# Reciprocal denominators expanded on TensorE instead of through DRAM, and transposes placed inside the key products

## The chip, the cores and the metric

The kernel runs on one core of a Trainium2 chip. The metric is the device time of one execution in microseconds; the number given for a kernel is the median of its runs. The engines are TensorE (PE in the profile; its weight loads are PEld), VectorE (DVE), ScalarE (ACT), GpSimd (POOL) and SyncE (SP), which here only issues DMAs.

## What is computed

x has 2048 rows (tokens) of 640 features. It is normalised over the features, and two branches read the result xn. Branch A is a linear attention with 32 heads of 20 features; branch B is a two-layer network with 1728 hidden units. The output is x + A * silu(B). The reference, cut to what matters:

```python
def A(xn, wqkv, wo):                       # S = 2048, D = 640, H = 32, Dh = 20
    q, k, v = split(xn @ wqkv)             # heads
    phi = lambda t: where(t > 0, t + 1, exp(t)) + 1e-6
    pq, pk = phi(q), phi(k)
    kv  = einsum("bhsd,bhse->bhde", pk, v)
    z   = einsum("bhsd->bhd", pk)
    num = einsum("bhqd,bhde->bhqe", pq, kv)
    den = einsum("bhqd,bhd->bhq", pq, z)[..., None] + 1e-6
    return merge_heads(num / den) @ wo
def B(xn, w1, w2):
    return maximum(xn @ w1, 0) @ w2
xn = layernorm(x)
out = x + A(xn, wqkv, wo) * silu(B(xn, w1, w2))
```

## The kernel before

Every operation is recorded by a small scheduler, `Sched`, in the order in which the Python code issues it. Each engine runs its own instructions strictly in that order. A wait is put in front of an operation where it reads what another engine or a DMA wrote, or overwrites what another still reads. There is no planner: where a call stands in the code is where its instructions stand on each engine. All DMAs go through SP's queue, in order too.

The work goes in these stages.

Start. Token tiles (128 rows, `t`) are loaded, `LN_stats` and `LN_norm` normalise them on VectorE into `xn`. Tiles 0 to 3 are transposed on TensorE against an identity (`transposes`, five products, line 413) and copied from PSUM by ScalarE (`xnT_copy`, line 418); tiles 4 to 15 are transposed by DMA. `K_mm(t, b)` (line 430) makes the keys of a tile: two halves of 320 columns (`a`), five contraction steps (`k`), ten products into the PSUM banks b and b+1. With a list of steps `ks` it issues only those, both halves of a step next to each other. `K_exp`, `K_relu` (ScalarE) and `K_fin` (VectorE) turn the keys into `pk`. `warm(n)` issues n small products whose result nobody reads.

Main loop. For each of four chunks of 512 tokens (`j`), 5 query blocks (line 482, 5 products of 512 columns, evicted into `pqT`) and 13 hidden blocks (line 505, likewise, into `hT`), in a ring of six PSUM banks; among them the stats, norms and key products of the next chunk's tiles. The last 64 hidden units are made by `H_half` (line 518) into `hTl`: chunk 2jp lies on partitions 0 to 63, chunk 2jp+1 on 64 to 127. POOL sums `pk` into `zacc` (line 442). In chunk 3 follow `z_split`, `z_col` after block n = 7 and `den` after block n = 9: `den` makes all denominators in one bank, with 20 products of line 593 that each use 32 columns of the array, so head h of chunk i lies on partition 32 i + h. VectorE adds 1e-6 (line 597) and takes reciprocals (line 601) into `rden`.

Reciprocals. `den` then stores `rden` to a DRAM scratch `rxd`, every head's row 20 times (4 DMAs, line 605). After the weights of the second layer, five DMAs (line 666) load it back by feature into `rx`, which takes the room of `xnT`. `divide(m)` (line 678) multiplies one block of 128 features of `pqT` by it on VectorE, for all 2048 tokens at once.

Second part. `G_block(k)` makes xn.T @ pk (32 products of 320 columns each, line 685; five blocks, banks 0 to 3), copied by ScalarE into `GT`. `kv_block` (line 697) multiplies by the value weights and VectorE masks off what lies outside the heads, into `kvp`, which POOL clears before (line 812). `W_block(m)` (line 712) folds the output weights in, into `wf`; its left half is evicted by ScalarE (line 716), its right half by VectorE (line 718).

Then the second layer `U(p)` for eight pairs of token tiles (line 751, two halves `n` of 320 output columns, 26 products each) and `s_tile(t)` (line 779, 10 products), which makes branch A's result of one tile. The last 64 hidden units enter by products of 64 rows (line 729), in which the two tiles of a pair use the two row halves of the array. They are issued eight at a time: four that end pair p (even), four that begin pair p+1. So the odd pairs end in full products, and Silu (line 747) of their first half can go as soon as that half is done. Silu writes `g_sb`, which lies in `xnT`'s room, and so also waits for the `divide`s that read there (`divs`). `ubanks` gives even pairs banks 4 to 7 and odd ones 0 to 3. A `hook` between the halves of U issues other work: kv in pair 0, W in pair 1, from then on the `s_tile`s of the pair two before; pair 7's hook issues those of pairs 5 and 6. The last pair's two tiles come at the end. VectorE multiplies by `g_sb` (line 793) and adds x (line 796), and SP stores the tile (line 799). A tile is one piece of 640 columns, or two of 320 with `last=True`, as both last tiles are.

Of the kernel before, what the change touches and what calls it, by code (L numbers as in the profile page):

```python
# [211 lines left out]
def bass_recurrent_scan__linear_attn_block__dense_activation_relu__prompt_kernel(  # L212
# [74 lines left out]
    ek = nc.alloc_sbuf_tensor("ek", [P, NEK, 2, D], bf)  # L287
    er = nc.alloc_sbuf_tensor("er", [P, NER, 2, 512], bf)
    ident = nc.alloc_sbuf_tensor("ident", [P, P], bf)
    mh = nc.alloc_sbuf_tensor("mh", [P, C, H], f32)  # L290
    zmat = nc.alloc_sbuf_tensor("zmat", [P, C, H], bf)
    zacc = nc.alloc_sbuf_tensor("zacc", [P, D], f32)
# [12 lines left out]
    rx = xnT  # L305
    rxd = nc.dram_tensor("rden_by_feature", [D, S], bf).ap()

    psT = nc.alloc_psum_tensor("psT", [P, 8 * 512], f32)
    ps = [psT[:, 512 * i:512 * (i + 1)] for i in range(8)]
# [60 lines left out]
    warm(36)  # L370

    def build_consts():
        sc.op("POOL", lambda eng: eng.memset(mh[:, :, :], 1.0), W=[("mh",)])
# [52 lines left out]
    def K_mm(t, b, ks=None):  # L426
        fns = []
        for a, k in ([(a, k) for a in range(2) for k in range(C)] if ks is None else [(a, k) for k in ks for a in range(2)]):
            if True:
                fns.append(lambda eng, a=a, k=k: eng.matmul(  # L430
                    ps[b + a][:, 0:HN], lhsT=xnT[:, k, tok(t)], rhs=wqk[:, k, D + HN * a:D + HN * (a + 1)],
                    start=(k == 0), stop=(k == C - 1)))
        wks = [0, 1] if ks is None else [0 if ks[0] < KS else 1]
# [120 lines left out]
    K_relu(1, 2)  # L554
    LN_stats(4)
    K_fin(0)
    K_mm(2, 0)
    K_exp(2, 0)
    K_relu(2, 0)
    LN_stats(5)  # L560
# [27 lines left out]
    def den():  # L588
# [76 lines left out]
    for c in range(C):  # L665
        dma("SP", lambda eng, c=c: eng.dma_start(rx[:, c, :], rxd[P * c:P * (c + 1), :]),
            R=[("rxd", i) for i in range(J)], W=[("rx", c)], extra=[lastW1])


    pr = [0]  # L670
# [3 lines left out]
        pr[0] += 1  # L674
        return b

    def divide(m):
        return sc.op("DVE", lambda eng: eng.tensor_tensor(out=pqT[:, m, :], in0=pqT[:, m, :], in1=rx[:, m, :], op=ALU.mult),  # L678
                     R=[("rx", m)] + [("pqT", i, m) for i in range(J)], W=[("pqT", i, m) for i in range(J)])

    def G_block(k, b):
        fns = []
# [23 lines left out]
    def W_block(m):  # L706
        b = nextp()
        cs = cs_of_m(m)
        fns = []
        for a in range(2):  # L710
            for ci, c in enumerate(cs):
                fns.append(lambda eng, a=a, c=c, ci=ci: eng.matmul(  # L712
                    ps[b + a][:, 0:HN], lhsT=kvp[:, c, P * m:P * (m + 1)], rhs=wo_sb[:, c, HN * a:HN * (a + 1)],
                    start=(ci == 0), stop=(ci == len(cs) - 1)))
        sc.group("PE", fns, R=[("wo",), ("kvz",)] + [("kv", c) for c in cs], W=[("ps", b), ("ps", b + 1)])
        sc.op("ACT", lambda eng: eng.activation(out=wf[:, m, 0:HN], in_=ps[b][:, 0:HN], func=ACTF.Copy),
              R=[("ps", b)], W=[("wf", m, 0)])
        sc.op("DVE", lambda eng: eng.tensor_copy(wf[:, m, HN:D], ps[b + 1][:, 0:HN]),
              R=[("ps", b + 1)], W=[("wf", m, 1)])

    pairs = [(4 * jj + q, 4 * jj + q + 4) for jj in (0, 2) for q in range(4)]

    def ubanks(p):
        return [4, 6] if p % 2 == 0 else [0, 2]

    def U_half(p, start):
        bs = ubanks(p)
        jp, q = pairs[p][0] // 8, pairs[p][0] % 4
        return [(lambda eng, u=u, n=n: eng.matmul(  # L729
            ps[bs[n] + u][:, 0:HN], lhsT=hTl[64 * u:64 * (u + 1), jp, P * q:P * (q + 1)],  # L730
            rhs=w2l[64 * u:64 * (u + 1), HN * n:HN * (n + 1)], start=start, stop=not start))
            for n in range(2) for u in range(2)]

    def U(p, hook):
        t0, t1 = pairs[p]
        bs = ubanks(p)
        odd = p % 2 == 1
        jp = t0 // 8
        Rh = [("hT", t // 4, f) for t in (t0, t1) for f in range(NF)] + [("w2", 0), ("w2", 1)]
        Rl = [("hTl", 0), ("hTl", 1), ("w2l", 0), ("w2l", 1)]  # L740

        def bk(n):
            return [("ps", bs[n]), ("ps", bs[n] + 1)]

        def silu(n):
            go = g_sb[:, t0:t0 + 5:4, HN * n:HN * (n + 1)]
            sc.op("ACT", lambda eng: eng.activation(out=go, in_=ps2(bs[n], HN), func=ACTF.Silu),  # L747
                  R=bk(n), W=[("g", t0, n), ("g", t1, n)], extra=[divs[c] for c in sorted({v // S for t in (t0, t1) for v in (D * t, D * t + D - 1)})])

        for n in range(2):  # L750
            fns = [(lambda eng, u=u, t=t, f=f, n=n: eng.matmul(  # L751
                ps[bs[n] + u][:, 0:HN], lhsT=hT[:, f, tok(t)], rhs=w2_sb[:, f, HN * n:HN * (n + 1)],
                start=(f == 0 and not odd), stop=(f == NF - 1 and odd)))
                for u, t in enumerate((t0, t1)) for f in range(NF)]
            if n == 0 or odd:
                sc.group("PE", fns, R=Rh, W=bk(n))
                sc.allow_unread.update(bk(n))
                if odd:
                    silu(n)
            else:  # L760
                sc.group("PE", fns + U_half(p, False), R=Rh + Rl, W=bk(0) + bk(1))
                b2 = ubanks(p + 1)
                W2 = [("ps", b2[i] + u) for i in range(2) for u in range(2)]
                sc.group("PE", U_half(p + 1, True), R=Rl, W=W2)
                sc.allow_unread.update(W2)
                silu(0)
                silu(1)
            if n == 0:
                hook()

    so = [0]

    def s_tile(t, last=False):
# [4 lines left out]
        for a in range(2):  # L778
            sc.group("PE", [(lambda eng, c=c, a=a: eng.matmul(  # L779
                ps[b + a][:, 0:HN], lhsT=pqT[:, c, tok(t)], rhs=wf[:, c, HN * a:HN * (a + 1)],  # L780
                start=(c == 0), stop=(c == C - 1))) for c in range(C)],
                R=[("pqT", i, c) for c in range(C)] + [("wf", c, a) for c in range(C)], W=[("ps", b + a)])

        def piece(lo, hi, pin, addE="DVE"):
            shp = "p (a n) -> p a n"
# [22 lines left out]
    lastG = None  # L808
    for k in range(C):
        lastG = G_block(k, gb[k % 2])  # L810
    divs = [divide(m) for m in range(2)]
    sc.op("POOL", lambda eng: eng.memset(kvp, 0.0), W=[("kvz",)], extra=[lastG])
    for jx in range(4):
        dma("SP", lambda eng, jx=jx: eng.dma_start(
            xre[:, 4 * jx:4 * jx + 4, :], x2[512 * jx:512 * (jx + 1), :].rearrange("(t p) n -> p t n", p=P)),
            W=[("xre", jx)], extra=[lastG])
    def kv_all():
        for c, b in enumerate((0, 1, 2, 3, 0)):
            kv_block(c, b)
        for m in range(2, C):  # L820
            divs.append(divide(m))

    def w_all():
        pr[0] = 2
        for m in range(C):
            pr[0] = 2 + m % 2
            W_block(m)

    def s_hook(ts, b0):
        def f():  # L830
            for i, t in enumerate(ts):
                pr[0] = b0 // 2 + i % 2
                s_tile(t)
        return f
# [6 lines left out]
    pr[0] = 2  # L841
    for t in pairs[7]:
        s_tile(t, last=True)

    sc.wait_all_dma("SP", list(range(nds[0])))

# [30 lines left out]
```

## Time and profile before

The median of three runs is 226.52 us (226.36 to 227.22).

| | us |
|---|---|
| the profiled execution's own time | 226.36 |
| its span | 224.9 |
| ScalarE busy | 88.5 (39%) |
| VectorE busy | 102.7 (46%) |
| TensorE's weight loads busy | 136.1 (61%) |
| HBM read, written | 15.65 MB, 5.24 MB |

Stages of the span, with the busy time of TensorE in each:

```profile
0.00:14.57 14.57, 12.76 (x115) 10.79 (x116) 9.32 (x28) 9.06 (x15) 4.41 (x17) 1.00 0.88 297
14.57:112.50 97.93, 97.93 (x533) 48.49 (x530) 62.13 (x114) 61.15 (x105) 36.35 (x43) 1.00 0.28 63
112.50:134.24 21.74, 21.74 (x162) 15.66 (x161) 1.72 (x2) 3.41 (x5) 0.00 (x0) 1.00 1.00 311
134.24:218.43 84.19, 83.93 (x641) 59.30 (x639) 26.54 (x42) 14.18 (x22) 2.76 (x1) 1.00 0.19 65
218.43:224.90 6.47, 2.88 (x22) 1.86 (x19) 3.00 (x8) 0.70 (x1) 0.00 (x0) 1.00 0.16 51
```

The columns are the stretch and its length, then busy time and number of instructions of TensorE, its weight loads, VectorE, ScalarE and POOL, the granted clock, the share of the DMA engines and GB/s. The stretches are the start up to the first query product; the main loop; the G blocks; the rest up to the last 20 products of `s_tile`; and the tail. The DMA engines are at their full share through the G blocks, when the weights of the second layer, the reciprocals and x are loaded. Such a table tells how full an engine is; what it waited for stands in the chain of waits and in the timeline, and a weight load beside a running product costs nothing of its own.

### The profile page before, as it was taken

Reading aid. Unit: us, or ns where it says so; the run is one execution under the profiler, and the core shown is the slowest. Engines: PE = TensorE matmul, PEld = TensorE weight load, DVE = VectorE, ACT = ScalarE, POOL = GpSimd, SP = SyncE. Lnnn points to the kernel's source line nnn. Section 1 sums busy time; section 2 is a strip of 40 time slices with the busy share of each in tenths; the row PEclk is TensorE's granted clock in tenths of the full one; section 3 lists DMA queues with packets and bytes.
Section 4 is the critical chain, followed back from the end, with each engine's and each line's share of the span. In section 5 each row is a group of like instructions: output and inputs, shape, how many; then the busy total and the mean of one; then the engine's idle time right before and its main releaser. Section 6 shows DMA issues by size and latency. Waiting matters only on the chain.

```text
span 224.9 us, 3511 instructions
## 1 busy us (share of the span) xinstructions
PE 219.2 (97%) x1464; PEld 136.1 (61%) x1464; DVE 102.7 (46%) x192; ACT 88.5 (39%) x147; POOL 43.5 (19%) x60
## 2 busy tenths in 40 slices
PE   7999999999999999999999999999999999999993
PEld 7754555455554555444477777667767767776772
DVE  3799921796639772967000044440404041331445
ACT  2798666656665666654521122241021102102110
POOL 2347642222442245700000004000000000000000
PEclk9999999999999999999999999999999999999999
DMA  6999800012101150000999999500001010101021
GB/s 207 326 395 257 223 12 0 0 31 58 32 1 29 30 56 5 0 3 0 205 218 292 338 398 325 184 0 3 30 28 61 0 60 3 58 0 61 26 91 58
DMA packets 24239, 23.07 MB, mean 103 GB/s; under 512 B 8992, under 2 KB 23584, under 8 KB 24224
## 3 DMA queue, kind: packets, MB, share of 16 engines
q1 hardware_dynamic: 24224, 22.86, 34.8%
q8 instruction: 11, 0.18, 0.4%
q14 instruction: 4, 0.03, 0.0%
HBM read 15.65 MB, written 5.24 MB: 93 GB/s over the span
## 4 chain that ended last, share of the span: by engine, by line
PE 94%; DVE 3%; ACT 1%; POOL 1%; issue 1%; POOLq 0%; DVEq 0%
PE psT L751 25%; PE psT L505 25%; PE psT L685 10%; PE psT L482 10%; PE psT L430 8%; PE psT L779 8%; PE psT L367 2%; PE psT L712 2%; PE psT L729 1%; PE psT L518 1%; DVE reg L793 1%; DVE stats L385 1%; PE psT L697 1%; PE psT L593 1%; DVE reg L796 0%
## 5 line engine op out<-in xcount | busy, mean ns | idle before, releaser
L751 PE MATMUL psT<-reg,hT 128*128 128x320 bf16 x416 | 58.7, 299 | 0.3
L505 PE MATMUL psT<-reg 128*128 128x512 bf16 x260 | 58.6, 379 | 0.0
L751 PEld LDWEIGHTS psT<-reg,hT 128*128 128x128 bf16 x416 | 40.3, 98 | 17.0 <-PE psT L729 1.6
L505 PEld LDWEIGHTS psT<-reg 128*128 128x128 bf16 x260 | 25.2, 98 | 29.2 <-ACT hT L509 0.4
L509 ACT ACTIVATE hT<-psT 128x512 bf16<-128x512 f32 x52 | 31.0, 599 | 18.6 <-PE psT L505 18.3
L747 ACT ACTIVATE reg<-psT 128x640 bf16<-128x640 f32 x16 | 10.8, 702 | 68.8 <-PE psT L729 35.4
L793 DVE TENSOR_TENSOR reg<-psT,reg 128x640 bf16<-128x640 f32 (+1 forms) x18 | 13.5, 749 | 49.0 <-PE psT L779 46.0
L442 POOL TENSOR_TENSOR zacc<-zacc,reg 128x640 f32<-128x640 f32 x16 | 22.6, 1410 | 22.6 <-DVE reg L461 22.3
L430 PE MATMUL psT<-reg 128*128 128x320 bf16 x160 | 24.4, 300 | 0.0
L779 PE MATMUL psT<-reg,pqT 128*128 128x320 bf16 x160 | 22.9, 299 | 0.0
L482 PE MATMUL psT<-reg 128*128 128x512 bf16 x100 | 22.2, 379 | 0.0
L685 PE MATMUL psT<-reg 128*128 128x320 bf16 x160 | 21.9, 299 | 0.0
L430 PEld LDWEIGHTS psT<-reg 128*128 128x128 bf16 x160 | 15.5, 98 | 8.0 <-ACT reg L418 0.2
L685 PEld LDWEIGHTS psT<-reg 128*128 128x128 bf16 x160 | 15.6, 98 | 6.4 <-issue 0.4
L779 PEld LDWEIGHTS psT<-reg,pqT 128*128 128x128 bf16 x160 | 15.7, 98 | 6.1
L678 DVE TENSOR_TENSOR pqT<-pqT,reg 128x2048 bf16<-128x2048 bf16 x5 | 5.9, 1220 | 26.8 <-DMA reg<-rden_by_feature 26.8
L482 PEld LDWEIGHTS psT<-reg 128*128 128x128 bf16 x100 | 9.8, 98 | 11.2
L385 DVE BATCH_NORM_STATS2 stats<-reg 128x6 f32<-128x320 bf16 x32 | 14.0, 480 | 3.3 <-DMA reg<-in_A_x_dram 3.3
L489 ACT ACTIVATE er<-psT 128x512 bf16<-128x512 f32 x20 | 12.2, 611 | 8.1 <-PE psT L482 3.5
L447 ACT ACTIVATE ek<-psT 128x640 bf16<-128x640 f32 x16 | 11.3, 707 | 9.1 <-PE psT L430 9.1
L459 DVE TENSOR_SCALAR ek<-ek 128x640 bf16<-128x640 bf16 x16 | 5.5, 343 | 19.3 <-ACT ek L447 19.3
L499 DVE SCALAR_TENSOR_TENSOR pqT<-er 128x512 bf16<-128x512 bf16 x15 | 12.9, 859 | 0.5
(58 smaller groups left out, 140.8 us busy)
## 6 DMA issues: line engine op xcount, KB each, us to landing
reg<-in_A_x_dram SPq DMA_DIRECT2D x16, 160.0 KB, 5.1
rden_by_feature<-rden SPq DMA_DIRECT2D x4, 640.0 KB, 8.7
reg<-rden_by_feature SPq DMA_DIRECT2D x5, 512.0 KB, 11.1
reg<-in_A_x_dram SPq DMA_DIRECT2D x4, 640.0 KB, 6.9
reg<-in_B_w_dram SPq DMA_DIRECT2D x2, 1120.0 KB, 9.9
out_dram<-reg SPq DMA_DIRECT2D x14, 160.0 KB, 1.8
reg<-in_B_w_dram SPq DMA_DIRECT2D x1, 1040.0 KB, 10.5
reg<-in_B_w_dram SPq DMA_DIRECT2D x1, 960.0 KB, 14.9
```

The costliest lines, as they stand in the source:

```text
L385: sc.op("DVE", lambda eng, a=a: eng.bn_stats(stats[:, t, a, :], xv[:, HN * a:HN * (a + 1)]), R=[("xin", t % XR)], W=[("stats", t, a)])
L430: fns.append(lambda eng, a=a, k=k: eng.matmul(ps[b + a][:, 0:HN], lhsT=xnT[:, k, tok(t)], rhs=wqk[:, k, D + HN * a:D + HN * (a + 1)], star ...
L442: sc.op("POOL", lambda eng: eng.tensor_tensor(out=zacc[:, :], in0=zacc[:, :], in1=pk[:, t, :], op=ALU.add), R=[("zacc",), ("pk", t)], W=[( ...
L482: sc.group("PE", [(lambda eng, k=k: eng.matmul(ps[b], lhsT=wqk[:, k, P * f:P * (f + 1)], rhs=xnT[:, k, schunk(j)], start=(k == 0), stop=(k ...
L489: sc.op("ACT", lambda eng: eng.activation(out=e_, in_=ps[b], func=ACTF.Exp), R=[("ps", b)], W=[("er_e", es)])
L499: sc.op("DVE", lambda eng: eng.scalar_tensor_tensor(out=pqT[:, f, schunk(j)], in0=e_, scalar=1.0, in1=r_, op0=ALU.min, op1=ALU.add), R=[(" ...
L505: a = sc.group("PE", [(lambda eng, k=k: eng.matmul(ps[b], lhsT=w1_sb[:, k, P * f:P * (f + 1)], rhs=xnT[:, k, schunk(j)], start=(k == 0), s ...
L509: sc.op("ACT", lambda eng: eng.activation(out=hT[:, f, schunk(j)], in_=ps[b], func=ACTF.Relu), R=[("ps", b)], W=[("hT", j, f)])
L685: fns.append(lambda eng, t=t, a=a: eng.matmul(ps[b + a][:, 0:HN], lhsT=xn[:, t, P * k:P * (k + 1)], rhs=pk[:, t, HN * a:HN * (a + 1)], sta ...
L751: fns = [(lambda eng, u=u, t=t, f=f, n=n: eng.matmul(ps[bs[n] + u][:, 0:HN], lhsT=hT[:, f, tok(t)], rhs=w2_sb[:, f, HN * n:HN * (n + 1)], ...
L779: sc.group("PE", [(lambda eng, c=c, a=a: eng.matmul(ps[b + a][:, 0:HN], lhsT=pqT[:, c, tok(t)], rhs=wf[:, c, HN * a:HN * (a + 1)], start=( ...
L793: sc.op("DVE", lambda eng: eng.tensor_tensor(out=tmpo[:, os_, lo:hi].rearrange(shp, a=na), in0=src, in1=g_sb[:, t, lo:hi].rearrange(shp, a ...
```

## The change

Six things change.

- `K_mm` of tiles 1 and 2 is issued in two parts, contraction steps 0 to 3 and step 4. The transposes of tile 2 stand between the parts of tile 1, and those of tile 3 between the parts of tile 2; before, both stood between the key products of tiles 1 and 2, as whole calls.
- The way through DRAM is gone: the stores to `rxd`, the loads of `rx`, and `divide`. Instead a 0/1 matrix `EmQ` (32 heads by 640 features, copied to four groups of 32 partitions) is set up on POOL in `build_consts`, and `expand(m)` multiplies it with `rden` on TensorE: four products of 32 rows and 512 columns, one for each chunk, into banks 4 to 7, one call after each `G_block`. VectorE multiplies `pqT` by each bank, 20 products of 512 columns.
- `z_col` and `den` stand after blocks 8 and 12 of the last chunk instead of 7 and 9.
- The products of 64 rows are issued four at a time, at the end of every pair, and both Silus of a pair follow them. Silu no longer waits for divisions.
- `W_block` evicts a whole block with one engine, in turns, and stands as a group of its own after U(0).
- The `s_tile`s come one pair behind U instead of two, and only the very last tile is split into two pieces.

```diff
     K_exp(0, 0)
     warm(4)
-    K_mm(1, 2)
+    K_mm(1, 2, range(0, 4))
     K_relu(0, 0)
     LN_norm(3)
     transposes(2, 6)
     xnT_copy(2, 6)
+    K_mm(1, 2, range(4, C))
     warm(4)
+    K_mm(2, 0, range(0, 4))
     transposes(3, 4)
     xnT_copy(3, 4)
     K_exp(1, 2)
     K_relu(1, 2)
     LN_stats(4)
     K_fin(0)
-    K_mm(2, 0)
+    K_mm(2, 0, range(4, C))
     K_exp(2, 0)
...
     def build_consts():
+        em = EmQ[0:H, :, :].rearrange("p c n -> p (c n)")
+        sc.op("POOL", lambda eng: eng.memset(em, 1.0), W=[("Em",)])
+        sc.op("POOL", lambda eng: eng.affine_select(out=em, in_=em, compare_op=ALU.is_ge, fill=0.0,
+                                                    base=0, pattern=[[1, D]], channel_multiplier=-DH),
+              R=[("Em",)], W=[("Em",)])
...
+        for qd in range(1, 4):
+            dma("SP", lambda eng, qd=qd: eng.dma_start(EmQ[H * qd:H * (qd + 1), :, :], EmQ[0:H, :, :]),
+                R=[("Em",)], W=[("Em4", qd)])
...
-        for i in range(J):
-            dma("SP", lambda eng, i=i: eng.dma_start(
-                rxd.rearrange("(h e) s -> h e s", e=DH)[:, :, schunk(i)],
-                rden[H * i:H * (i + 1), :].unsqueeze(1).to_broadcast([H, DH, 512])), R=[("rden",)], W=[("rxd", i)])
...
-                if n == 7:
+                if n == 8:
                     z_col()
-                if n == 9:
+                if n == 12:
                     den()
...
-    def divide(m):
-        return sc.op("DVE", lambda eng: eng.tensor_tensor(out=pqT[:, m, :], in0=pqT[:, m, :], in1=rx[:, m, :], op=ALU.mult),
-                     R=[("rx", m)] + [("pqT", i, m) for i in range(J)], W=[("pqT", i, m) for i in range(J)])
+    def expand(m):
+        fns = [(lambda eng, i=i: eng.matmul(ps[4 + i], lhsT=EmQ[H * i:H * (i + 1), m, :], rhs=rden[H * i:H * (i + 1), :],
+                                            start=True, stop=True)) for i in range(J)]
+        sc.group("PE", fns, R=[("rden",), ("Em",)] + [("Em4", q) for q in range(1, 4)], W=[("ps", 4 + i) for i in range(J)])
+        for i in range(J):
+            sc.op("DVE", lambda eng, i=i: eng.tensor_tensor(out=pqT[:, m, schunk(i)], in0=pqT[:, m, schunk(i)],
+                                                            in1=ps[4 + i], op=ALU.mult),
+                  R=[("ps", 4 + i), ("pqT", i, m)], W=[("pqT", i, m)])
...
-    def U(p, hook):
+    def U(p, hook=None):
         t0, t1 = pairs[p]
-        bs = ubanks(p)
+        bs = [nextp(), nextp()]
...
+        for n in range(2):
+            for u in range(2):
+                fns.append(lambda eng, u=u, n=n: eng.matmul(
+                    ps[bs[n] + u][:, 0:HN], lhsT=hTl[64 * u:64 * (u + 1), jp, P * q:P * (q + 1)],
+                    rhs=w2l[64 * u:64 * (u + 1), HN * n:HN * (n + 1)], start=False, stop=True))
+        sc.group("PE", fns, R=Rh + [("hTl", jp), ("w2l", 0), ("w2l", 1)],
+                 W=[("ps", bs[n] + u) for n in range(2) for u in range(2)])
+        for n in range(2):
             go = g_sb[:, t0:t0 + 5:4, HN * n:HN * (n + 1)]
+            sc.op("ACT", lambda eng, go=go, n=n: eng.activation(out=go, in_=ps2(bs[n], HN), func=ACTF.Silu),
+                  R=[("ps", bs[n]), ("ps", bs[n] + 1)], W=[("g", t0, n), ("g", t1, n)])
...
     for k in range(C):
         lastG = G_block(k, gb[k % 2])
-    divs = [divide(m) for m in range(2)]
+        expand(k)
...
+    pr[0] = 1
     U(0, kv_all)
-    U(1, w_all)
-    for p in range(2, 8):
-        ts = pairs[p - 2] if p < 7 else pairs[5] + pairs[6]
-        U(p, s_hook(ts, 0 if p % 2 == 0 else 4))
-    pr[0] = 2
+    pr[0] = 3
+    for m in range(C):
+        W_block(m)
+    for p in range(1, 8):
+        a, b = pairs[p - 1]
+        if p == 1:
+            U(p)
+            s_tile(a)
+            s_tile(b)
+        elif p < 7:
+            U(p, lambda: s_tile(a))
+            s_tile(b)
+        else:
+            U(p, lambda: (s_tile(a), s_tile(b)))
+    pr[0] += 2
     for t in pairs[7]:
-        s_tile(t, last=True)
+        s_tile(t, last=(t == pairs[7][1]))
```

More of the change, by code (lines that the diff above doesn't have):

```diff
@@ L289, in bass_recurrent_scan__linear_attn_block__dense_activation_relu__prompt_kernel @@
     ident = nc.alloc_sbuf_tensor("ident", [P, P], bf)
+    EmQ = nc.alloc_sbuf_tensor("EmQ", [P, C, P], bf)
     mh = nc.alloc_sbuf_tensor("mh", [P, C, H], f32)
@@ L303, in bass_recurrent_scan__linear_attn_block__dense_activation_relu__prompt_kernel @@
     rsy = nc.alloc_sbuf_tensor("rsy", [P, T], f32)
-    rx = xnT
-    rxd = nc.dram_tensor("rden_by_feature", [D, S], bf).ap()
     psT = nc.alloc_psum_tensor("psT", [P, 8 * 512], f32)
@@ L372, in build_consts @@
     def build_consts():
+        em = EmQ[0:H, :, :].rearrange("p c n -> p (c n)")
[3 more added lines that the diff above has]
+              R=[("Em",)], W=[("Em",)])
+        sc.op("POOL", lambda eng: eng.affine_select(out=em, in_=em, compare_op=ALU.is_ge, fill=0.0,
+                                                    base=DH - 1, pattern=[[-1, D]], channel_multiplier=DH),
+              R=[("Em",)], W=[("Em",)])
+        for qd in range(1, 4):
+            dma("SP", lambda eng, qd=qd: eng.dma_start(EmQ[H * qd:H * (qd + 1), :, :], EmQ[0:H, :, :]),
+                R=[("Em",)], W=[("Em4", qd)])
         sc.op("POOL", lambda eng: eng.memset(mh[:, :, :], 1.0), W=[("mh",)])
@@ L432, in K_mm @@
                     start=(k == 0), stop=(k == C - 1)))
-        wks = [0, 1] if ks is None else [0 if ks[0] < KS else 1]
+        wks = [0, 1] if ks is None else sorted({0 if k < KS else 1 for k in ks})
         sc.group("PE", fns, R=[("xnT", t)] + [("wk", i) for i in wks], W=[("ps", b), ("ps", b + 1)])
@@ L664, in bass_recurrent_scan__linear_attn_block__dense_activation_relu__prompt_kernel @@
     w_load(wo_sb, A_wo, ("wo",), extra=[last_norm[0]])
-    for c in range(C):
-        dma("SP", lambda eng, c=c: eng.dma_start(rx[:, c, :], rxd[P * c:P * (c + 1), :]),
-            R=[("rxd", i) for i in range(J)], W=[("rx", c)], extra=[lastW1])
     pr = [0]
@@ L715, in W_block @@
         sc.group("PE", fns, R=[("wo",), ("kvz",)] + [("kv", c) for c in cs], W=[("ps", b), ("ps", b + 1)])
[L716 to L719, printed above, removed]
-    pairs = [(4 * jj + q, 4 * jj + q + 4) for jj in (0, 2) for q in range(4)]
-    def ubanks(p):
-        return [4, 6] if p % 2 == 0 else [0, 2]
@@ L726, in U_half @@
-    def U_half(p, start):
-        bs = ubanks(p)
[L728 to L732, printed above, removed]
-    def U(p, hook):
+        if m % 2 == 0:
+            sc.op("ACT", lambda eng: eng.activation(out=wf[:, m, :].rearrange("p (a n) -> p a n", a=2), in_=ps2(b, HN),
+                                                    func=ACTF.Copy), R=[("ps", b), ("ps", b + 1)], W=[("wf", m)])
+        else:
+            sc.op("DVE", lambda eng: eng.tensor_copy(wf[:, m, :].rearrange("p (a n) -> p a n", a=2), ps2(b, HN)),
+                  R=[("ps", b), ("ps", b + 1)], W=[("wf", m)])
@@ L735, in U @@
+    pairs = [(4 * jj + q, 4 * jj + q + 4) for jj in (0, 2) for q in range(4)]
+    def U(p, hook=None):
         t0, t1 = pairs[p]
-        bs = ubanks(p)
-        odd = p % 2 == 1
+        bs = [nextp(), nextp()]
         jp = t0 // 8
+        q = t0 % 4
         Rh = [("hT", t // 4, f) for t in (t0, t1) for f in range(NF)] + [("w2", 0), ("w2", 1)]
[L740 to L745, printed above, removed]
-            go = g_sb[:, t0:t0 + 5:4, HN * n:HN * (n + 1)]
-            sc.op("ACT", lambda eng: eng.activation(out=go, in_=ps2(bs[n], HN), func=ACTF.Silu),
-                  R=bk(n), W=[("g", t0, n), ("g", t1, n)], extra=[divs[c] for c in sorted({v // S for t in (t0, t1) for v in (D * t, D * t + D - 1)})])
@@ L750, in U @@
[L750 to L769, printed above, removed]
+        for n in range(2):
+            fns = []
+            for u, t in enumerate((t0, t1)):
+                for f in range(NF):
+                    fns.append(lambda eng, u=u, t=t, f=f, n=n: eng.matmul(
+                        ps[bs[n] + u][:, 0:HN], lhsT=hT[:, f, tok(t)], rhs=w2_sb[:, f, HN * n:HN * (n + 1)],
+                        start=(f == 0), stop=False))
+            if n == 0:
+                sc.group("PE", fns, R=Rh, W=[("ps", bs[0]), ("ps", bs[0] + 1)])
+                sc.allow_unread.update([("ps", bs[0]), ("ps", bs[0] + 1)])
+                if hook is not None:
+                    hook()
@@ new lines, in U @@
+        for n in range(2):
[5 more added lines that the diff above has]
+                 W=[("ps", bs[n] + u) for n in range(2) for u in range(2)])
+        for n in range(2):
+            go = g_sb[:, t0:t0 + 5:4, HN * n:HN * (n + 1)]
+            sc.op("ACT", lambda eng, go=go, n=n: eng.activation(out=go, in_=ps2(bs[n], HN), func=ACTF.Silu),
+                  R=[("ps", bs[n]), ("ps", bs[n] + 1)], W=[("g", t0, n), ("g", t1, n)])
@@ L781, in s_tile @@
                 start=(c == 0), stop=(c == C - 1))) for c in range(C)],
-                R=[("pqT", i, c) for c in range(C)] + [("wf", c, a) for c in range(C)], W=[("ps", b + a)])
+                R=[("pqT", i, c) for c in range(C)] + [("wf", c) for c in range(C)], W=[("ps", b + a)])
         def piece(lo, hi, pin, addE="DVE"):
@@ L817, in kv_all @@
     def kv_all():
-        for c, b in enumerate((0, 1, 2, 3, 0)):
+        b0, b1 = nextp(), nextp()
+        for c, b in enumerate((b0, b0 + 1, b1, b1 + 1, b0)):
             kv_block(c, b)
-        for m in range(2, C):
-            divs.append(divide(m))
-    def w_all():
-        pr[0] = 2
[L825 to L834, printed above, removed]
-    U(0, kv_all)
-    U(1, w_all)
-    for p in range(2, 8):
-        ts = pairs[p - 2] if p < 7 else pairs[5] + pairs[6]
-        U(p, s_hook(ts, 0 if p % 2 == 0 else 4))
-    pr[0] = 2
+    pr[0] = 1
+    U(0, kv_all)
+    pr[0] = 3
[10 more added lines that the diff above has]
+            s_tile(b)
+        else:
+            U(p, lambda: (s_tile(a), s_tile(b)))
+    pr[0] += 2
     for t in pairs[7]:
-        s_tile(t, last=True)
+        s_tile(t, last=(t == pairs[7][1]))
     sc.wait_all_dma("SP", list(range(nds[0])))
```

## The prediction

> **What bounds the kernel now.** I read the page's busy shares and slices first, then the chain that ended last, then the starts of single matmuls at the places that the change touches.
>
> ```profile
> span 224.9 us, 3511 instructions
> ...
> PE 219.2 (97%) x1464; PEld 136.1 (61%) x1464; DVE 102.7 (46%) x192; ACT 88.5 (39%) x147; POOL 43.5 (19%) x60
> ...
> PEclk9999999999999999999999999999999999999999
> ...
> PE 94%; DVE 3%; ACT 1%; POOL 1%; issue 1%; POOLq 0%; DVEq 0%
> ...
> L678 DVE TENSOR_TENSOR pqT<-pqT,reg 128x2048 bf16<-128x2048 bf16 x5 | 5.9, 1220 | 26.8 <-DMA reg<-rden_by_feature 26.8
> ```
>
> TensorE is busy for 97% of the span at the full granted clock and carries 94% of the chain. The 26.8 us that VectorE waits for the replicated reciprocals is on no path: TensorE never waits for VectorE in that stretch. So what counts is TensorE time, plus the start before its unbroken run and the tail behind it. The chain in the stretch where the denominators and the second layer are made (start, duration, what):
>
> ```profile
> 100.35 1.19 PE psT L593 x20
> ...
> 112.56 21.84 PE psT L685 x160
> 134.40 3.53 PE psT L751 x26
> ...
> 151.00 7.06 PE psT L751 x52
> ```
>
> A full matmul of 320 columns takes 3.53/26 = 0.136 us. One of 512 columns takes 0.216 (4.32 us for 20 in the chain of line 505). The 20 products of line 593 take only 1.19 us: four that use different 32-column parts of the array run side by side. The timeline of TensorE around one block of 64-row products (line 729), and at the start:
>
> ```profile
> 142.46 0.57 PE L751 MATMUL psT<-reg,hT 128*128 128x320 bf16 x3
> 142.96 0.72 PE L729 MATMUL psT<-reg,hTl 64*128 64x320 bf16 x8
> 143.74 0.31 PE L751 MATMUL psT<-reg,hT 128*128 128x320 bf16 x1
> ```
>
> ```profile
> 9.24 1.53 PE L430 MATMUL psT<-reg 128*128 128x320 bf16 x10
> 10.61 0.44 PE L413 MATMUL psT<-ident,reg 128*128 128x128 bf16 x5
> ...
> 11.46 0.45 PE L413 MATMUL psT<-ident,reg 128*128 128x128 bf16 x5 [0.19 <-DVE reg L403]
> 11.84 2.89 PE L430 MATMUL psT<-reg 128*128 128x320 bf16 x20
> 14.57 0.38 PE L482 MATMUL psT<-reg 128*128 128x512 bf16 x1
> ```
>
> The last 128-row matmul starts at 142.46 + 2 x 0.136 = 142.73, the first 64-row one at 142.96, the last at 143.38 (its end, 143.68, less its 0.296), and the next 128-row one at 143.74. The eight take four steps of 0.136, so the two row halves run side by side. Entering costs 0.23 - 0.136 = 0.09 us and leaving 0.36 - 0.136 = 0.22. With about 0.01 for the slower first step a visit to split rows costs s = 0.33 us beside its columns; the whole block costs 143.74 - 142.73 - 0.136 = 0.88.
>
> **The sum goes part by part, against the profiled execution's own 226.36 us (span 224.9, 1.46 around it); the median of the runs shown is 226.52.**
>
> **Start.** No work is added; the transposes of tiles 2 and 3 move. Before, tile 2's transposes start at 10.61 and their copy on ScalarE at 11.08 (0.47 later, 0.70 long); tile 3's start at 11.46, held by its norm (line 403, 10.96 + 0.45), with the copy at 11.95. The key products of tiles 2 and 3 then run without a gap from 11.84 to 14.57, when the queries start. After: 8 of 10 products of tile 1 end their issue at 9.24 + 8 x 0.136 = 10.33 (tile 2's norm is done at 10.24), so tile 2's transposes start 0.27 earlier, the copy runs 10.81 to 11.51, and the first 8 products of tile 2 start at 11.57 (0.06 after a copy's end, as at 11.84). Now tile 3's transposes stand behind those 8 instead of ahead of them: 11.57 + 0.01 + 1.09 = 12.67 instead of 11.46. Their copy runs 13.15 to 13.85. The two last products of tile 2 cover only to 13.22, so tile 3's products start at 13.91 and the queries at 13.91 + 1.37 = 15.28: **+0.71 us**. Queued behind that copy on ScalarE are the exponentials of tiles 1 to 3, about 1.2 us later; VectorE's K_fin(1) waits for them, 0.6 us later. Who waits for those is the eviction of the query blocks, and a ring of six banks (6.5 us of TensorE) separates them from TensorE. From 11.84 on TensorE has no gap in which lost time could be won back, so it all stays. Bounds: 0 if tile 3 were covered after all, 1.1 if the queries wait for ScalarE too (the 1.2 us less the slack already there).
>
> **Expansion of the reciprocals.** Removed: four stores and five loads on SP's queue and five products on VectorE (5.9 us), none on a path. Added on TensorE: after each of five G blocks, four products of 32 rows by 512 columns. No row shows four row groups at once. From below: side by side, no cost of the switch, 5 x 0.216 = 1.1. From above: one after another, 5 x (4 x 0.216 + 0.33) = 6.0. I take side by side with the switch, 5 x (0.216 + 0.33) = **+2.74 us**, because the nearest rows, two row halves (line 729) and four column quarters (line 593), both run fully side by side. The Trainium skill, "TensorE: Matmul & The Clock Gate", Part 3, gives 3.07 times for four such products instead of 4; by that figure, as an estimate, each group takes 0.28 and the time would be 231.9.
>
> VectorE gets 20 products from PSUM of 128x512. The row of line 597 (128x512 from PSUM) says 0.69 us, so 2.76 us a block; a G block gives 4.34 us, so the banks 4 to 7 are free again 1.6 us ahead. The last block's four end 2.8 us after their expansion, 0.7 ahead of the kv products (3.53 us later, after the first half of U(0)) that reuse banks 6 and 7. If the memset of kvp on POOL (2.76 us, same time) held VectorE up, that wait would be up to 1.8 us; line 497, which reads PSUM too, keeps its 0.67 us beside POOL's adds, so I take 0.
>
> **Setting up EmQ, and the later z_col and den.** One memset and two selects on POOL at 83.6. By the rows of 363 and 374 (0.63 us, and 0.36 for a quarter of the elements) 0.63 + 2 x 1.44 = 3.5 us at most. POOL's next two adds slip, but the third waits until 91.3 for its tile anyway, so z_split does not move. The three DMAs of EmQ have 30 us to land, and nothing stands behind them on SP before 112.6. den moves three H blocks on: 3.2 us; its 0.69 + 3.35 us on VectorE end near 110, and the first expansion is at 117.6. All 0; without that cover any lateness would count one for one.
>
> **Split-row blocks in the second layer.** The same 32 products of line 729 come as eight blocks of four instead of four of eight. One block of four: 2 x 0.136 + 0.33 = 0.606. Eight are 4.85, four of before 4 x 0.878 = 3.51: **+1.34 us**. If a visit cost nothing it would be 2.18 - 3.51 = -1.33; if the two halves did not overlap, 8 x (0.54 + 0.33) - 3.51 = +3.5. I take the row itself: it is the same product. The rule that speaks against this change is in the Trainium skill's "TensorEngine Tiling (Array Packing)", Key Properties: "Mode switching requires drain". The page has no price for it; by it alone thirteen visits instead of four are dearer, and the measured gaps agree with the rule. Banks: every U now uses 0 to 3 and every s_tile 4 to 7. U(p+1) writes bank 0 no sooner than 1.36 us after U(p), and Silu (0.60 a step) has read it by 1.04 us. W's third block finds banks 2 and 3 read 0.6 us ahead. So no wait; without that slack each pair would lose up to 0.7.
>
> **Tail.** Before, from the first of the last 20 products (line 779, 218.43) to the end of the last add (222.25 + 0.33) is 4.14 us: only one Silu (half) is left, and four half-tile pieces on VectorE. After, two Silus are left, but tile 7a's single full piece waits for its ten products: 1.58 us after that first product. Then 0.86 + 0.50 (full product and add, as at 160.31 and 160.81), 0.53 + 0.24 + 0.52 and 0.33 for the two half pieces: 4.56. **+0.42 us**; bounds 0.2 and 0.8 (one step of VectorE either way).
>
> Sum: 0.71 + 2.74 + 1.34 + 0.42 = 5.2; 226.36 + 5.2 = 231.6 us.
>
> **Rivals.** (1) Four row groups do not run side by side: each expansion takes 0.65 us more, 3.2 in all, 234.8. For it: no row shows four. Against it: lines 593 and 729. (2) The start loses nothing, because tile 3's copy is covered or the late queries are made good: 230.9. Against it: TensorE has no gap after 11.84. (3) Not slower: the gaps around line 729 belong to that block (new weights, banks just freed), not to the change of rows. Then s is near 0, the split rows gain 1.33, the expansions cost 1.1, and 0.71 + 1.08 - 1.33 + 0.42 = 0.9 remains: 227.3, within 0.5%. It decides where 13 s is under about 0.24, that is s under 0.02. Against it: line 593 shows gaps of 0.09 on both sides too, with other operands. (4) VectorE is held up behind POOL's memset and the kv products wait: 1.8 more, 233.4.
>
> **How the numbers follow.** My case has 0.78, with its own range of 230.6 to 232.6 (start 0 to 1.1 and tail 0.2 to 0.8 rarely go the same way). Rival 1 has 0.06, rival 2 0.08, rival 3 0.04, rival 4 0.04. The range of 230.2 to 233.4 holds my case and rivals 2 and 4 and leaves out 1 and 3, 0.10, and as much again for what I do not see. About 0.5%, 1.1 us, is what a measurement of this kernel can tell from no change. Slower 0.95; within 0.5% 0.04 (rival 3); faster 0.01, since only several terms together would have to turn.
>
> **What would show it.** Queries start near 15.3 us with a gap of about 0.6 ahead of tile 3's key products. Each expansion shows four starts within some 0.01 us and 0.55 us between the G blocks around it. Eight visits to line 729's products of 0.6 us. The last add ends 4.6 us after the first of the last 20 products. The prediction is wrong where the four starts stand 0.2 us apart, where s differs, or where a bank makes TensorE wait.

## The result, and the profile after

The changed kernel takes 230.25 us (median of five runs, 229.98 to 230.78) against 226.54 for the kernel before. The ratio is 1.0158 (95% interval 1.0137 to 1.0179), so it is slower by 3.1 to 4.1 us. The forecast was slower by 5.2. The direction was right, and so were the four places where time was lost; one wait was missed, the loss is over a quarter smaller than foretold, and the time lies at the lower edge of the range of 230.2 to 233.4 (the ratio, put on the 226.52 us shown ahead of the prediction, gives 230.1).

The page of the changed kernel shows the same picture as before: TensorE at full clock, 97% busy, on nearly the whole chain. The loads and stores of the reciprocals are gone from the DMA engines, and nothing got faster by it.

```profile
span 228.5 us, 3562 instructions
...
PE 222.1 (97%) x1484; PEld 134.9 (59%) x1484; DVE 108.2 (47%) x202; ACT 88.1 (39%) x145; POOL 45.7 (20%) x63
...
PE 95%; ACT 2%; DVE 1%; issue 0%; POOL 0%; POOLq 0%
```

Where the time went is read by cutting both timelines at the same four instructions (us; profiled executions):

| stretch | before | after | difference |
|---|---|---|---|
| start of the span to the key products of tile 1 | 9.24 | 9.36 | +0.12 |
| from there to the first query product | 5.33 | 6.04 | +0.71 |
| queries and hidden blocks, to the first G product | 97.92 | 97.93 | 0.00 |
| G, second layer, tiles, to the first of the last 20 products | 105.94 | 108.62 | +2.69 |
| from there to the end of the last add | 4.14 | 4.44 | +0.30 |
| last store and end | 2.34 | 2.09 | -0.25 |

These make up the spans' difference of 3.56. The first row goes with the landing of x's second tile, which the change does not touch (VectorE's statistics of it start at 5.41 before, at 5.74 after). The last row is no gain: the two profiled executions differ by 3.89 us, 0.33 more than their spans, and in all ten profiles of this case an end that is 0.25 shorter comes with about 0.3 more outside the span. The other three are the change: 3.70 us.

The start of the changed kernel, TensorE's timeline:

```profile
9.36 1.26 PE L439 MATMUL psT<-reg 128*128 128x320 bf16 x8 [0.21 <-ACT reg L427]
10.45 0.44 PE L422 MATMUL psT<-ident,reg 128*128 128x128 bf16 x5
10.73 0.43 PE L439 MATMUL psT<-reg 128*128 128x320 bf16 x2
11.00 0.39 PE L365 MATMUL psT<-ident 128*128 128x128 bf16 x4
11.69 1.26 PE L439 MATMUL psT<-reg 128*128 128x320 bf16 x8 [0.30 <-ACT reg L427]
12.79 0.44 PE L422 MATMUL psT<-ident,reg 128*128 128x128 bf16 x5
13.07 0.43 PE L439 MATMUL psT<-reg 128*128 128x320 bf16 x2
14.03 1.53 PE L439 MATMUL psT<-reg 128*128 128x320 bf16 x10 [0.52 <-ACT reg L427]
15.39 0.59 PE L491 MATMUL psT<-reg 128*128 128x512 bf16 x2
```

Tile 3's transposes (12.79) stand behind eight key products of tile 2, and tile 3's key products wait for ScalarE's copy: the bracket of 0.52 at 14.03. Nothing after 15.39 wins this back.

One expansion between two G blocks, and one block of four 64-row products:

```profile
117.27 0.57 PE L694 MATMUL psT<-reg 128*128 128x320 bf16 x3
117.77 0.40 PE L682 MATMUL psT<-rden,EmQ 32*128 32x512 bf16 x4
118.10 0.31 PE L694 MATMUL psT<-reg 128*128 128x320 bf16 x1
```

```profile
157.03 0.30 PE L744 MATMUL psT<-reg,hT 128*128 128x320 bf16 x1
157.26 0.45 PE L754 MATMUL psT<-reg,hTl 64*128 64x320 bf16 x4
157.64 0.31 PE L772 MATMUL psT<-reg,pqT 128*128 128x320 bf16 x1
```

The four 32-row products start within 0.40 - 0.39 = 0.01 us of each other, so they run side by side, and a G block with its expansion takes 4.78 us where one without took 21.74 / 5 = 4.35: 0.43 a visit, not 0.55. The last of the 64-row products starts at 157.26 + 0.45 - 0.30 = 157.41, and the next full product 0.23 later. In the kernel before this step out took 0.36.

### The profile page after: what moved, and what is told of

It is laid out like the page before. It is cut to its first block, busy times and chain, and to the rows that moved or that the text cites. A ratio compares the mean times of both kernels' runs of the same rounds, so it can differ in the third digit from the quotient of the medians.

```text
span 228.5 us, 3562 instructions
## 1 busy us (share of the span) xinstructions
PE 222.1 (97%) x1484; PEld 134.9 (59%) x1484; DVE 108.2 (47%) x202; ACT 88.1 (39%) x145; POOL 45.7 (20%) x63
## 4 chain that ended last, share of the span: by engine, by line
PE 95%; ACT 2%; DVE 1%; issue 0%; POOL 0%; POOLq 0%
PE psT L744 25%; PE psT L514 25%; PE psT L694 10%; PE psT L491 9%; PE psT L772 9%; PE psT L439 9%; PE psT L365 2%; PE psT L721 2%; PE psT L754 1%; ACT reg L427 1%; PE psT L527 1%; DVE reg L786 1%; PE psT L682 1%; PE psT L706 1%; ACT L542 1%; PE psT L604 1%
## 5 line engine op out<-in xcount | busy, mean ns | idle before, releaser
L439 PE MATMUL psT<-reg 128*128 128x320 bf16 x160 | 24.9, 299 | 1.1 <-ACT reg L427 1.0
L772 PE MATMUL psT<-reg,pqT 128*128 128x320 bf16 x160 | 23.9, 299 | 0.0
L694 PE MATMUL psT<-reg 128*128 128x320 bf16 x160 | 22.6, 299 | 0.0
L686 DVE TENSOR_TENSOR pqT<-pqT,psT 128x512 bf16<-128x512 bf16 x20 | 12.4, 682 | 17.7 <-PE psT L682 17.7
L772 PEld LDWEIGHTS psT<-reg,pqT 128*128 128x128 bf16 x160 | 15.1, 98 | 7.4 <-issue 1.8
```

The costliest lines, as they stand in the source:

```text
L439: fns.append(lambda eng, a=a, k=k: eng.matmul(ps[b + a][:, 0:HN], lhsT=xnT[:, k, tok(t)], rhs=wqk[:, k, D + HN * a:D + HN * (a + 1)], star ...
L694: fns.append(lambda eng, t=t, a=a: eng.matmul(ps[b + a][:, 0:HN], lhsT=xn[:, t, P * k:P * (k + 1)], rhs=pk[:, t, HN * a:HN * (a + 1)], sta ...
L772: sc.group("PE", [(lambda eng, c=c, a=a: eng.matmul(ps[b + a][:, 0:HN], lhsT=pqT[:, c, tok(t)], rhs=wf[:, c, HN * a:HN * (a + 1)], start=( ...
```

## The experiments

Two theories stood against each other on that step. **W**: in the kernel before, 0.13 of the 0.36 us was TensorE waiting for its own last group, and changing from full to split rows costs only about 0.1 us each way. **R**: leaving split rows costs 0.22 us by itself, as the prediction had it. W has a source in the scheduler. It collects the last writer of every bank that a group overwrites, whichever engine that was:

```python
        for key in W:
            st = self.res.get(key)
            if st is not None:
                if st.w is not None:
                    agents.append(st.w)
```

What an engine itself has done counts as known only once it has waited for it, so TensorE is made to wait for the end of its own group when the next one writes the same banks. In the kernel before, the second four of the eight products write the banks of the next pair, and the next group is that pair's. Such a wait stands in the lists of waits of both kernels, before and after:

```profile
PEld psT L751 <- PE psT L729: 1.6, 4, 0.4
```

```profile
PEld psT L744 <- PE psT L744: 0.4, 1, 0.4
```

(engine that waited, for whom: us in total, times, longest). The second has no split rows at all: it lies between the two halves of pair 1, the only pair that has no other work between them.

### The start alone

```diff
...
-    K_mm(1, 2)
+    K_mm(1, 2, range(0, 4))
...
     xnT_copy(2, 6)
+    K_mm(1, 2, range(4, C))
     warm(4)
+    K_mm(2, 0, range(0, 4))
     transposes(3, 4)
...
-    K_mm(2, 0)
+    K_mm(2, 0, range(4, C))
```

> The kernel before with the start of the changed kernel alone: key products of tiles 1 and 2 in two parts, with the transposes of tiles 2 and 3 inside. Theory: the transposes of tile 3 stand behind eight key products of tile 2, their copy ends 1.2 us later, TensorE stands idle for about 0.6 us ahead of the key products of tile 3, and the queries start 0.71 us later (15.28 instead of 14.57); nothing behind makes it good, so the time is 0.7 us over the kernel before. Rival: the slack of the query blocks takes it up, and the time is that of before within 0.2 us.

Measured: 227.24 us, ratio 1.0032 (1.0020 to 1.0044), 0.72 us more. In its profile the key products of tile 1 start at 10.00, since x's second tile landed later (statistics at 6.38 instead of 5.41); from there to the queries (16.04) it is 6.04 us instead of 5.33, and everything behind takes what it took before. (The trace lacks the first query product here and in the runs below; its start is put at that of the last key product plus 0.136.) The theory holds; the rival falls.

### The order of the two fours

```diff
-                sc.group("PE", fns + U_half(p, False), R=Rh + Rl, W=bk(0) + bk(1))
+                sc.group("PE", fns, R=Rh, W=bk(1))
+                sc.allow_unread.update(bk(1))
...
                 sc.group("PE", U_half(p + 1, True), R=Rl, W=W2)
                 sc.allow_unread.update(W2)
+                sc.group("PE", U_half(p, False), R=Rl, W=bk(0) + bk(1))
```

> The kernel before with one order changed: of the eight 64-row products, the four that begin the next pair are issued ahead of the four that end this one. Nothing is added or taken away. Theory W: the 0.36 us from the last 64-row product to the next full one are TensorE's wait for its own last group, since the scheduler makes it wait where the next group writes the same banks; with four other products between, the step out falls to 0.23 us at each of the four blocks, 0.13 x 4 = 0.52 us less than the kernel before. Rival R: leaving split rows costs 0.22 us by itself; then the step out stays at 0.36 and the time is that of before.

Measured: 225.99 us, ratio 0.9979 (0.9970 to 0.9987), 0.53 us less. TensorE's timeline around the first of the four blocks:

```profile
142.61 0.57 PE L751 MATMUL psT<-reg,hT 128*128 128x320 bf16 x3
143.11 0.72 PE L729 MATMUL psT<-reg,hTl 64*128 64x320 bf16 x8
143.76 0.31 PE L751 MATMUL psT<-reg,hT 128*128 128x320 bf16 x1
```

The block is as long as before (0.72), and the next full product starts 143.76 - (143.11 + 0.72 - 0.30) = 0.23 us after the last 64-row one. That is before the last 64-row product has ended by the trace (143.83); in the kernel before, the next full product came 0.06 us after that end (143.68 to 143.74). So 0.13 us of each step out was TensorE's wait for itself. R falls: the same products, rows and banks, in another order, leave for 0.09 us over the 0.136 of a full step. The list of waits still names line 729, since the next pair waits for the four that are now issued first, but with 1.1 us instead of 1.6:

```profile
PEld psT L729 <- issue: 1.1, 4, 0.3
PEld psT L751 <- PE psT L729: 1.1, 4, 0.3
```

What is left, 0.27 us each, is as long as the idle time of the weight loads on the way into line 729, where no wait is named.

### Tile 3's transposes put back

```diff
     warm(4)
-    K_mm(2, 0, range(0, 4))
     transposes(3, 4)
...
-    K_mm(2, 0, range(4, C))
+    K_mm(2, 0)
```

> The changed kernel with the transposes of tile 3 ahead of all ten key products of tile 2 again; the transposes of tile 2 stay inside the key products of tile 1. Theory: only the second move costs; the first one gains about 0.1 us, since tile 2's copy is ready earlier. Queries start near 14.5 to 14.7 us instead of 15.39, and the time is 0.8 us under the changed kernel. Rival: both moves cost, or what costs is that the key products come in two parts; then less than 0.4 us comes back.

Measured: 229.44 us, ratio to the kernel before 1.0131 (1.0117 to 1.0144), 0.81 us under the changed kernel. TensorE's timeline:

```profile
10.51 0.44 PE L422 MATMUL psT<-ident,reg 128*128 128x128 bf16 x5
10.79 0.43 PE L439 MATMUL psT<-reg 128*128 128x320 bf16 x2
11.06 0.39 PE L365 MATMUL psT<-ident 128*128 128x128 bf16 x4
11.66 0.45 PE L422 MATMUL psT<-ident,reg 128*128 128x128 bf16 x5 [0.21 <-DVE reg L412]
11.95 2.88 PE L439 MATMUL psT<-reg 128*128 128x320 bf16 x20
```

With tile 2's transposes still inside tile 1's products, the way from the key products of tile 1 (9.41) to the queries (14.66) is 5.25 us, 0.09 less than before. So the two moves have opposite signs: tile 2's gains 0.09, tile 3's costs 0.79. The split of tile 1's products, which is still there, shows no cost.

### The expansion alone

```diff
+    def expand(m):
...
-        return [4, 6] if p % 2 == 0 else [0, 2]
+        return [2, 0] if p % 2 == 0 else [4, 6]
...
         lastG = G_block(k, gb[k % 2])
-    divs = [divide(m) for m in range(2)]
+        expand(k)
...
-        for c, b in enumerate((0, 1, 2, 3, 0)):
+        for c, b in enumerate((6, 7, 4, 5, 6)):
```

(with `EmQ`, and without the stores, the loads and the waits of Silu for the divisions, as in the change; W's and the tiles' banks are swapped likewise)

> The kernel before with the expansion of the reciprocals on TensorE in place of the way through DRAM, and nothing else; so that VectorE can read banks 4 to 7, even pairs use banks 0 to 3 and odd ones 4 to 7, and kv, W and the tiles swap banks likewise. The start, the blocks of eight 64-row products and the tail are those of before. Theory W: five visits of 0.22 us of columns and 0.21 for the change of rows, 2.15 us over the kernel before. Rival R (0.33 a visit): 2.7 us over. Rival: the loads of reciprocals that go free something, and it is under 1.5 us.

Measured: 228.66 us, ratio 1.0093 (1.0080 to 1.0106), 2.14 us more. From the first G product to the first of the last 20 it takes 108.10 us against 105.94: 2.16 more, five times 0.43 (4.45 + 0.33 a block in its chain of waits, where 4.35 stood):

```profile
112.55 4.45 PE psT L692 x32
117.00 0.33 PE psT L680 x4
117.33 4.45 PE psT L692 x32
121.78 0.33 PE psT L680 x4
```

The way through DRAM cost the kernel before nothing that this one gets back.

### The order of the second layer alone

```diff
-    def U(p, hook):
+    def U(p, hook=None):
...
-    U(1, w_all)
-    for p in range(2, 8):
-        ts = pairs[p - 2] if p < 7 else pairs[5] + pairs[6]
-        U(p, s_hook(ts, 0 if p % 2 == 0 else 4))
+    for m in range(C):
+        W_block(m)
+    for p in range(1, 8):
+        a, b = pairs[p - 1]
...
```

(U, W and the loop over the pairs as in the changed kernel; Silu keeps its waits for the divisions)

> The kernel before with the changed kernel's second layer alone: 64-row products in eight blocks of four, both Silus behind each pair, W by itself, the tiles one pair behind, one whole last piece; the start and the way through DRAM are those of before. Theory W: eight blocks at 0.475 us instead of four at 0.878 are 0.29 more, TensorE's wait for its own group inside pair 1 is 0.22, the tail 0.30: 0.8 us over the kernel before. By the prediction's price of 0.606 a block: 1.34 + 0.42 = 1.8 us over.

Measured: 227.61 us, ratio 1.0045 (1.0032 to 1.0057), 1.10 us more, 0.3 over what W expects. In the profile the stretch from G to the last 20 products is 106.46 us against 105.94, +0.52, and the tail 4.44 against 4.14, +0.30: the 0.82 that W expects. In this profile the rest lies ahead of the edit: x's second tile was ready 0.63 us later (VectorE's statistics of tile 1 at 6.04 instead of 5.41), and the key products of tile 1 start 0.43 later (9.66 instead of 9.24). Why that landing was late, and whether it was so in the other four runs, isn't settled. The price of 0.606 a block falls either way.

### Another end of pair 7

```diff
...
+        sc.group("PE", full(0), R=Rh, W=bk(0))
...
+        hook()
+        sc.group("PE", half(1), R=Rl, W=bk(1))
+        sc.group("PE", half(0), R=Rl, W=bk(0))
+        silu(0)
+        sc.group("PE", full(1), R=Rh, W=bk(1))
+        silu(1)
...
-        s_tile(t, last=(t == pairs[7][1]))
+        s_tile(t, last=True)
```

> The changed kernel with another end of pair 7: its four 64-row products between the halves, so that Silu of the first half goes early and full products end the pair, and both last tiles in two pieces, as before. Theory: from the first of the last 20 products to the end of the last add 4.14 us as before instead of 4.44, so 0.3 us under the changed kernel. Rival: the tail is VectorE's four steps whatever is done ahead of them, and nothing changes.

Measured: 229.91 us, 0.34 under the changed kernel's median; the intervals of the two ratios (1.0135 to 1.0162 and 1.0137 to 1.0179) overlap, so the time alone does not decide it. The profile does: the tail is 4.14 us. The chain's last part, first of the changed kernel and then of this one (whose line 772 is not `s_tile`, but the full products of pair 7):

```profile
221.63 0.38 PE psT L754 x4
222.01 1.48 PE psT L772 x10
223.49 0.02 issue
223.51 0.84 DVE reg L786
```

```profile
218.41 3.65 PE psT L772 x26
222.07 0.02 issue
222.09 0.71 ACT reg L788
```

In the changed kernel VectorE's last stretch begins when ten products of a whole tile are done (1.57 us after the first); here it begins behind one Silu. The rival falls.

### Work between the halves of pair 1

```diff
         if p == 1:
-            U(p)
-            s_tile(a)
+            U(p, lambda: s_tile(a))
             s_tile(b)
```

> The changed kernel with one tile of pair 0 between the two halves of pair 1, as in the later pairs. No row change lies between these halves. Theory W: the 0.36 us from one full product to the next there are TensorE's wait for its own group and go to 0.14, 0.22 us less. Rival: what holds the second half is a bank that ScalarE or VectorE still reads; then the gap stays or moves to the new place.

Measured: one time, 229.79 us. From G to the last 20 products 108.39 us instead of 108.62: 0.23 less. There is no wait of line 744 for itself in its list any more. In the changed kernel the second half of pair 1 starts at 153.27 + 0.67 - 0.31 = 153.63, 0.36 us after the last product of the first half:

```profile
153.27 0.67 PE L744 MATMUL psT<-reg,hT 128*128 128x320 bf16 x2
```

In this one TensorE goes on without a pause:

```profile
152.13 1.25 PE L744 MATMUL psT<-reg,hT 128*128 128x320 bf16 x8
153.22 1.52 PE L772 MATMUL psT<-reg,pqT 128*128 128x320 bf16 x10
```

This is W without any change of rows: the wait is between two groups of full products, and other work between them covers it.

### A version faster than both

It is the kernel before with the new order of the two fours, and with the transposes of tile 2 inside the key products of tile 1.

> The kernel before with two things that the runs point to: the four 64-row products of the next pair ahead of the four of this one, and the transposes of tile 2 inside the key products of tile 1 (tile 3's stay ahead of tile 2's products). Theory: 0.52 less by the first, 0.1 less by the second: 0.6 us under the kernel before, 225.9. Rival for the second: norm 3 sets the start, and only 0.5 is left.

Measured: 225.84 us, ratio to the kernel before 0.9969 (0.9959 to 0.9980), 0.7 us less and 4.4 less than the changed kernel. From the key products of tile 1 to the queries it takes 5.25 us, from G to the last 20 products 105.40 instead of 105.94. The first of the change's two moves in the start is thus good for 0.09 us; the second costs nearly nine times that.

## Why the prediction was wrong, and where it was right

By the sum's own terms (us):

| term | predicted | measured | by |
|---|---|---|---|
| start | +0.71 | +0.71 | timelines, the start alone (0.72) |
| five expansions | +2.74 | +2.17 | the 2.69 of the timelines less the 0.52 below; the expansion alone (2.14) |
| split-row blocks | +1.34 | +0.52 | timeline of the second layer alone: 0.30 for the blocks, 0.22 for the wait in pair 1 |
| tail | +0.42 | +0.30 | timelines, the other end of pair 7 |
| sum | +5.2 | +3.70 | |

**The step that failed is s = 0.33 us, the price of a visit to split rows.** It was read from line 729 as 0.09 in, 0.22 out and 0.01. The way in was right. The way out held 0.13 us of another thing, TensorE's wait for its own group, which the order of the two fours made and which the new blocks and the expansions don't have. With 0.20 in place of 0.33, a block of four costs 0.47 and an expansion 0.42 to 0.43. That takes 0.57 from the expansions and 1.04 from the blocks, 1.6 together, where 1.5 lay between the sum and the measured loss; the missed wait below gave 0.22 of it back. The sign was there to be seen: the lines 593 and 518 left their split columns for 0.09, the list of waits named line 729 as what line 751's weights waited for, and I took the larger gap for the nature of rows instead of asking what stood in it. Rival 3 came close: it held that the gaps belong to that block, with "banks just freed" as a reason. It was half true, for 0.13 of the 0.33, and far from the s under 0.02 at which it would have decided.

**A wait was missed.** The forecast said that no bank makes TensorE wait in the new order; it counted the engines that read a bank and left out TensorE's own writes. The halves of pair 1 have no work between them, and the second half's group writes the first's banks too: 0.22 us, found by the same rule of the scheduler and taken away by one tile in between.

**The start** was right step by step: the copy, the idle time ahead of tile 3's key products and the queries. Rival 2 falls. What the forecast did not separate is that the two moves differ in sign.

**Four row groups** run side by side, as assumed; rival 1 (3.2 us more) falls. The Trainium skill's figure of 3.07 times ("TensorE: Matmul & The Clock Gate", Part 3) is under what this kernel shows. From the first start of an expansion to the next G product it is 0.33 us; less 0.10 for the way out that is 0.23, where one product of 512 columns takes 0.216: 4 x 0.216 / 0.23 = 3.8 times.

**The Trainium skill's rule that a change of tiling drains the array** ("TensorEngine Tiling (Array Packing)", Key Properties) pointed the right way: each change costs time. Its measured size here is about 0.1 us a change, in the swapped kernel as in the changed one; that a drain is the cause, no run here shows.

**VectorE and POOL** were free, as costed. The four products of an expansion take 2.48 us beside POOL's memset (137.34) as without it (118.22), so rival 4 falls:

```profile
118.22 2.48 DVE L686 TENSOR_TENSOR pqT<-pqT,psT 128x512 bf16<-128x512 bf16 x4 [8.48 <-PE psT L682]
...
137.34 2.48 DVE L686 TENSOR_TENSOR pqT<-pqT,psT 128x512 bf16<-128x512 bf16 x4 [2.30 <-PE psT L682]
```

Each takes 0.62 us in a row instead of the 0.69 assumed. Setting up `EmQ` went into POOL's slack: `z_split` starts 0.83 us later than before, as much as the queries do. The main loop's 97.93 us against 97.92 show that it and the later `den` cost nothing.

**The tail** was 0.12 too dear: a half piece follows a whole add after 0.41 us (224.37 to 224.78), not after the 0.50 taken from a pair of whole pieces:

```profile
224.37 0.49 DVE L789 TENSOR_TENSOR reg<-reg 128x640 bf16<-128x640 bf16 x1
224.78 0.48 DVE L786 TENSOR_TENSOR reg<-psT,reg 128x320 bf16<-128x320 f32 x1
```

The parts add up: 0.72 + 2.14 + 1.10 = 3.96 us by the medians of the three parts alone, 0.71 + 2.16 + 0.82 = 3.69 by their profiles, and the whole is 3.71 by the medians. The 0.27 between the two sums of parts is nearly all in the second layer alone (1.10 against 0.82).

## What to carry to other kernels

Before a gap in a trace is taken for the price of an operation, look at what is waited for in it, and find a second place with the same operation and other neighbours; one number of 0.13 us, used thirteen times, makes 1.7 us, and the forecast was 1.5 too high. An in-order engine can be made to wait for itself by a scheduler that treats its own writes like another engine's; put work on other banks between such groups, or order them so that the next group's banks were written earliest. Transposes inside a product stream pay only as far as what follows them covers the copy out of PSUM: tile 2's gained 0.09 us, tile 3's, moved behind eight products with two left to cover its copy, cost 0.79.

## What the runs showed of the hardware that I had not expected

Leaving row-split products costs no more than entering them: about 0.09 to 0.10 us over a full step either way, for two halves of 320 columns and for four quarters of 512.

The time at which x's second tile has landed differs by 1 us between profiles of kernels that are the same up to there (VectorE's statistics of tile 1 start between 5.41 and 6.38 us). From 5.74 us on it moves the key products of tile 1 one for one (5.74 to 9.36, 6.38 to 10.00); ahead of that it hardly does (5.41 to 9.24). TensorE has no gap behind the start, so a late start of these products stays in the span. They start between 9.18 and 10.00 us, and that spread is more than several of the effects measured here, which is why they are read from stretch to stretch and not from the spans.
